# A fused linear-attention and expert layer: one count-table fill moved behind the last unit, the gate weights loaded later, the first expert's weights loaded once

## The chip, the cores and the metric

The kernel runs on one core of a Trainium2 chip. The metric is the device time of one launch in microseconds (us); lower is better. The core has a matrix engine (TensorE, PE in the profile), VectorE (DVE), ScalarE (ACT), GpSimd (POOL) and SyncE (SP). SP and POOL also start transfers; POOL starts all that need an address from a register or from a list of rows.

## The reference

Gated linear attention over 4 sequences of 768 steps and 8 heads of size 48, then a layer of 8 experts on the 3072 tokens (384 numbers each), each expert taking exactly 384 tokens.

```python
# attention
for t in range(S):
    state = alpha[:, :, t, :, None] * state + einsum('bhd,bhe->bhde', k[:, :, t], v[:, :, t])
    y[:, :, t] = einsum('bhd,bhde->bhe', q[:, :, t], state)
# experts: the largest logits first, one expert a token, cap = N / E tokens an expert
logits = x @ w_gate
for idx in argsort(-logits.flatten()):
    tok, e = idx // E, idx % E
    if assigned[tok] < 0 and counts[e] < cap: assigned[tok] = e; counts[e] += 1
for e in range(E):
    out[assigned == e] = relu(x[assigned == e] @ w1[e]) @ w2[e]
```

## The kernel before

**Attention.** The work is cut into 24 units: 6 chunks of 128 steps of each of 4 sequences, all 8 heads in a unit. `loads(n)` brings in alpha, k, q and v of unit n on SP's queue (L345 to L348). In `unit(n)` VectorE runs a product scan over alpha backwards (L366, then a reciprocal, L368) and forwards (L371) and multiplies k by the one (L376); q is multiplied by the other (L381), by VectorE in unit 0 and by GpSimd in all later units. TensorE transposes the scaled k (L394), makes the scores (L404), k times v (L418) and the two products of the output (L442: the carried state, and the scores with v). ScalarE copies the scores out of PSUM (L408) in two halves, `sm`, of four heads each, and GpSimd sets the future half of each to zero (L410). ScalarE copies out the output (L457), and TensorE makes its 8 logits with `wg` and `sel` (L463, L468). Unit 0 is worked in two halves. A few products on zeros (L266) run at the start.

**Choice of tokens.** Instead of sorting, the kernel finds in 7 rounds the expert that fills next and the smallest logit that still gets in: a logit is split in 5 digits (7, 7, 6, 6 and 6 bits), and for each digit VectorE compares all tokens' digits with a ramp (L712, into a count table `cmp`, two buffers `cbuf`, 128 columns a digit value), TensorE counts (L695, L700), and VectorE picks the digit (L698, L703). A digit of 6 bits fills 64 of the 128 columns, yet the counting products read all 128, so that the rest has to hold numbers. `round_(i)` ends in `ei`, the number of expert i (L746), and in a list of its tokens (L837 to L847), with which GpSimd gathers their rows (L854).

**Experts.** Each float32 number is worked as a high and a low part in fp32r, with three products in place of one: high by high, low by high and high by low (L961 for w1, L992 for w2). A quarter of an expert's weights (`g` = 0 to 3, 768 KB, w1 in the first half of its columns and w2 in the second) is loaded by two transfers on GpSimd's queue: `hi` (L875) writes the rounded number, ScalarE writes its negative into the place of the low part in two halves (L885), and `low` (L889) loads the same 768 KB again and adds it to that. ffn1 has to wait for `hi` for its first two products and for `low` for its third. Two sets of buffers take turns (`WS`). The second set lies where the attention's output was.

**What sets the order.** Every step is an `op` with an engine, an estimated length, a due time and what it has to follow; `plan` sorts them once, when the program is built, and each engine then works its list strictly in that order. So a step that waits holds up all that stands behind it on its engine. GpSimd's list mixes transfers, masks and products; SP's holds the loads.

The constants (ramps, shifts, masks, the tables `iotas`, `ramp_b`) are made by the lists `INIT` and `LATE`; there GpSimd fills both `cbuf` with zeros (L322, six steps). For the first expert `second(0)` writes its own order, `hi` and `low` by turns, behind the gathers.

## Time and profile before

| | |
|---|---|
| time, median of 3 runs | 412.94 us (412.81 to 415.25) |
| the profiled execution's own time | 415.02 us |
| its span, first to last instruction | 413.0 us |
| PE, DVE, ACT, POOL busy | 383.0, 258.3, 173.5, 186.1 us |
| mean granted TensorE clock, as a share of the full one | 0.966 |

The rows come from the profiled execution, which is 2.1 us above the median. Times in rows count from its first instruction. Attention takes the first 113 us, the first choice of tokens and the handover go to 147, and the experts to the end. A granted clock of 1.00 is 2.4 GHz, 0.50 is 1.2 GHz.

### The profile page before, as it was taken

To read this page: it belongs to the slowest core of one execution; us is meant where nothing else is said; L and a number is where in the kernel's file an instruction comes from. 1 tells how busy PE (TensorE), PEld (TensorE's weight loads), DVE (VectorE), ACT (ScalarE), POOL (GpSimd) and SP (SyncE) were. 2 spreads that over 40 slices of the span, in tenths; PEclk is the share of its full clock that TensorE was granted. 3 is DMA by queue.
4 is the path that set the end of the run, shared out by engine and by line. 5 is a ranking of instruction groups with operands and counts; after the bars stand their busy time and mean duration, and the time that the engine had idled before them with its cause. 6 is when DMAs were issued, how large, how long until landed. Compare 5 with 4: busy or idle time off the path is not lost.

```text
span 413.0 us, 10416 instructions
## 1 busy us (share of the span) xinstructions
PE 383.0 (93%) x4166; PEld 341.1 (83%) x4166; DVE 258.3 (63%) x649; ACT 173.5 (42%) x320; POOL 186.1 (45%) x271
## 2 busy tenths in 40 slices
PE   6699999999989758899999999999999999999991
PEld 3578787878767447799999999999999999999990
DVE  7699999995557854656956955956865753221110
ACT  4255555556464133424362552551461372553110
POOL 9777876678400421611550660560550473431202
PEclk9699999999998986899999999999999999999997
DMA  7996878940054579998999989889889899999101
GB/s 204 391 340 201 259 236 273 289 136 5 4 193 172 151 202 253 255 306 174 288 283 215 303 201 211 256 235 207 230 267 201 220 326 208 322 272 195 64 0 57
DMA packets 30176, 88.82 MB, mean 215 GB/s; under 512 B 4144, under 2 KB 10544, under 8 KB 30128
## 3 DMA queue, kind: packets, MB, share of 16 engines
q0 software_dynamic: 12288, 59.78, 56.2%
q1 hardware_dynamic: 17840, 28.39, 20.6%
q8 instruction: 32, 0.52, 0.5%
q14 instruction: 16, 0.13, 0.1%
HBM read 78.72 MB, written 9.44 MB: 213 GB/s over the span
## 4 chain that ended last, share of the span: by engine, by line
PE 74%; issue 8%; POOL 5%; DVE 5%; DMA 4%; ACT 1%; POOLq 0%; ACTq 0%
PE h L961 20%; PE y L992 20%; PE y L442 9%; PE s L404 6%; PE xt L695 6%; DMA wset<-in_w_dram 4%; PE xt L394 2%; PE xt L418 2%; PE xt L463 2%; PE xt L928 2%; PE xt L468 2%; POOL out_dram L1006 1%; PE xt L843 1%; POOL cmp L322 1%; DVE hot L837 1%
## 5 line engine op out<-in xcount | busy, mean ns | idle before, releaser
L992 PE MATMUL y<-wset,hh 128*128 128x384 f32 x384 | 102.8, 349 | 0.0
L961 PE MATMUL h<-xh,wset 128*128 128x384 f32 x384 | 92.3, 350 | 5.7 <-DMA wset<-in_w_dram 5.7
L972 ACT ACTIVATE hh<-h 128x384 fp32r<-128x384 f32 x64 | 31.4, 490 | 120.1 <-PE h L961 107.5
L974 DVE SCALAR_TENSOR_TENSOR hl<-h,hh 128x384 fp32r<-128x384 f32 x64 | 35.5, 554 | 65.1 <-ACT hh L972 64.8
L961 PEld LDWEIGHTS h<-xh,wset 128*128 128x128 f32 x384 | 68.9, 193 | 7.1 <-issue 5.0
L992 PEld LDWEIGHTS y<-wset,hh 128*128 128x128 f32 x384 | 68.2, 191 | 0.0
L992 PE MATMUL y<-wset,hl 128*128 128x384 f32 x192 | 65.1, 339 | 0.0
L885 ACT ACTIVATE wset<-wset 128x768 fp32r<-128x768 f32 x64 | 50.7, 839 | 15.1 <-DMA wset<-in_w_dram 14.8
L875 POOL DMA_DIRECT2D wset<-in_w_dram x32 | 21.0, 670 | 67.7 <-PE h L961 39.6
L854 POOL DMA_INDIRECT xr<-x_dram,idx x24 | 25.7, 1070 | 53.9 <-DVE dig L786 27.5
L889 POOL DMA_DIRECT2D wset<-in_w_dram x32 | 29.7, 1154 | 40.5 <-ACT wset L885 39.6
L961 PE MATMUL h<-xl,wset 128*128 128x384 f32 x192 | 45.7, 346 | 0.0
L410 POOL TENSOR_SCALAR_AFFINE_SELECT sm<-sm 128x512 f32<-128x512 f32 x48 | 32.9, 702 | 19.8 <-ACT sm L408 16.6
L1006 POOL DMA_INDIRECT out_dram<-yo,idx x24 | 27.2, 1134 | 30.5 <-ACT yo L1000 22.1
L695 PEld LDWEIGHTS <-cmp 128*128 128x128 bf16 x816 | 30.2, 118 | 10.2 <-DVE cmp L712 5.8
L992 PEld LDWEIGHTS y<-wset,hl 128*128 128x128 f32 x192 | 36.5, 190 | 0.0
L408 ACT ACTIVATE sm<-s 128x512 f32<-128x512 f32 x48 | 26.9, 596 | 18.6 <-PE s L404 17.7
L961 PEld LDWEIGHTS h<-xl,wset 128*128 128x128 f32 x192 | 34.3, 192 | 0.0
L712 DVE TENSOR_TENSOR cmp<-nd,iota 128x1536 bf16<-128x1536 bf16 (+2 forms) x32 | 32.7, 1032 | 1.0
L381 POOL TENSOR_TENSOR qh<-qr,ga 128x512 f32<-128x512 f32 x23 | 29.8, 1295 | 4.8 <-issue 1.8
L695 PE MATMUL xt<-oc,cmp 128*128 128x8 bf16 x720 | 28.9, 175 | 2.3 <-DVE cmp L712 2.3
L442 PE MATMUL y<-sm,vr 128*48 128x128 f32 x384 | 26.8, 283 | 4.0 <-POOL sm L410 4.0
(160 smaller groups left out, 579.1 us busy)
## 6 DMA issues: line engine op xcount, KB each, us to landing
wset<-in_w_dram POOLq DMA_DIRECT2D x64, 768.0 KB, 9.1
kr<-in_k_dram SPq DMA_DIRECT2D x24, 256.0 KB, 4.5
qr<-in_q_dram SPq DMA_DIRECT2D x24, 256.0 KB, 4.6
al<-in_alpha_dram SPq DMA_DIRECT2D x23, 258.5 KB, 4.2
vr<-in_v_dram SPq DMA_DIRECT2D x24, 192.0 KB, 3.5
x_dram<-xga SPq DMA_DIRECT2D x24, 192.0 KB, 1.9
xr<-x_dram,idx POOLq DMA_INDIRECT x24, 3.8
out_dram<-yo,idx POOLq DMA_INDIRECT x24, 6.5
```

The source lines that it names most:

```text
L381: (V if n == 0 else G).tensor_mul(qh[:, ps_], qr[:, ps_], ga[:, lo:hi].rearrange("p (g x) -> p g x", x=C1)[:, :, 1:])
L410: op("POOL", 0.65, lambda h=h: G.affine_select(sm[:, h], sm[:, h], pattern=[[0, HP], [1, C]], compare_op=OP.is_ge, fill=0.0, base=0, chann ...
L442: P_.matmul(yv[64 * g:64 * g + D, h, s], lhs, rhs, start=(h, g) not in fresh, stop=last and s == 1, skip_group_check=True)
L695: P_.matmul(rt_c, cmp_[:, j // U, :, j % U], o[:, j], start=j == 0, stop=j == NU - 1, skip_group_check=True)
L712: x = op("DVE", (1.75 if nt == 128 else 0.95) / n + 0.03, lambda js=js: V.tensor_tensor(words(cbuf[t % 2], nt, js), keyed(d, nt, js), each ...
L885: pre.append(op("ACT", 0.84, lambda hs=hs: A.activation(WS[i % 2][:, 1, g][:, hs], WS[i % 2][:, 0, g][:, hs].bitcast(F32), AF.Copy, scale= ...
L889: accs[i, g] = op("POOL", 0.92, lambda: nc.gpsimd.dma_start(WS[i % 2][:, 1, g], w12.bitcast(F32R)[bass.ds(eng_reg[i], 1), :, g].rearrange( ...
L961: P_.matmul(o, WS[i % 2][:, a, g, c0 + d * 128:c0 + (d + 1) * 128], x[:, d], start=m_ == 0 and d == 0, stop=m_ == 2 and d == DB - 1)
L972: a_ = op("ACT", 0.49, lambda: A.activation(HHT[m], o, AF.Relu), after=[y], r=[("hb", n_)], w=[("hh", n_)], at=at, boost=25, lat=0.1)
L974: op("DVE", 0.54, lambda: V.scalar_tensor_tensor(HLT[m], o, 0.0, HHT[m], op0=OP.max, op1=OP.subtract), after=[a_], r=[("hb", n_), ("hh", n ...
L992: P_.matmul(YB[b][:, :Dm], a[:, bs], w, start=q == 0 and n == 0, stop=q == FB - 1 and n == 2)
L1006: st_ = nc.gpsimd.indirect_dma_start(out=out, out_offset=bass.IndirectOffsetOnAxis(ap=IDX[i][:, b:b + 1], axis=0), in_=YO[c % 5], in_offse ...
```

## The change

Six things are changed.

1. The six fills of `cbuf` at the start are gone. One fill, of columns 64 to 127 of the first buffer, stands behind the masks of the last unit. (The second buffer's first use writes all 128 columns.)
2. The two loads of `wg` stand behind the loads of unit 1 on SP's queue, as a step of their own.
3. In unit 0 q is multiplied by GpSimd too, and k ahead of the forward scans; the products of its two score halves with v are two steps.
4. The tables `iotas` and `ramp_b` are made by VectorE elsewhere: `iotas` in units 0 and 1, `ramp_b` behind the scaled k of unit 6.
5. For the first expert each quarter is loaded once, as it is, into one of four new buffers (`RAW`); ScalarE writes the high part from it (two halves), and VectorE subtracts to make the low part (two halves). The halves are separate steps, so that w1's products do not wait for w2's half. All other experts are loaded as before. The first expert's four transfers stand in a row.
6. Estimated lengths of loads and fills are changed in the planner, which moves other steps by places.

```diff
+WG_AT, Q_DVE, K0_AT = -1.4, (), -0.05
+BY_DVE = ((0, 1, 2, 3), ())
...
     def wgate():
         V.memset(wg, 0.0)
+        V.tensor_reduce(sel, ident.rearrange("p (i e) -> p e i", e=32)[:, :E], axis=X_, op=OP.add)
+
+    def wgate_load():
         for h in range(2):
             nc.sync.dma_start(wg[64 * h:64 * h + D, :, :E],
                               w_gate.rearrange("(b h d) e -> h d b e", h=2, d=D)[h])
...
+    c_wg = op("DVE", 0.3, wgate, at=-4.0)
+    op("SP", 0.87, wgate_load, after=[c_wg], w=[("wg", 0)], at=WG_AT, dma=1.0, lat=1.0)
...
-    for c_ in cbuf:
-        for w_ in range(0, NW, 2):
-            LATE.append(("POOL", 0.6, lambda c_=c_, w_=w_: G.memset(c_[:, w_:w_ + 2], 0.0)))
...
-                (V if n == 0 else G).tensor_mul(qh[:, ps_], qr[:, ps_],
+                (V if n in Q_DVE else G).tensor_mul(qh[:, ps_], qr[:, ps_],
...
+    op("POOL", 1.45, lambda: G.memset(cbuf[0][:, :, 64:], 0.0), after=lastw["sm", NU - 1], at=NU + 5.0)
...
         def hi(g, after, follow=()):
...
+            raw = g in BY_DVE[i > 0]
...
+            x = op("POOL", 0.58, lambda: nc.gpsimd.dma_start(
+                t, w12[bass.ds(eng_reg[i], 1), :, g].rearrange("e p f -> p (e f)")), after=after, follow=follow,
+                w=[("raw", k)], at=at, dma=2.0, lat=LH if i else 0.5)
+            for h in range(2):
+                hs = slice(h * WB // 2, (h + 1) * WB // 2)
+                his[i, g, h] = op("ACT", 0.84, lambda hs=hs: A.activation(WS[i % 2][:, 0, g][:, hs], t[:, hs], AF.Copy),
...
+            for h in range(2):
+                hs = slice(h * WB // 2, (h + 1) * WB // 2)
+                accs[i, g, h] = op("DVE", 0.87, lambda hs=hs: V.tensor_sub(
+                    WS[i % 2][:, 1, g][:, hs], t[:, hs], WS[i % 2][:, 0, g][:, hs].bitcast(F32)),
...
     def second(i):
         hi, low, x = late_w.pop()
         rows = [gathers[i, NB - 1]]
-        if i == 0:
-            for g in range(GP):
-                hi(g, [x], rows)
-                rows = [his[0, g]]
-                if g:
-                    low(g - 1, rows)
-                    rows = [accs[0, g - 1]]
-            low(GP - 1, rows)
...
```

GpSimd's list at the start, before: `cmp` are the two count tables, `sm` the score halves of units 0, 1 and 2, `qh` the scaled q of units 1 and 2.

```order
L318 AFFINE_SELECT tri<-one_82 128x128
L322 MEMSET cmp_96 128x1024 x3
L322 MEMSET cmp_97 128x1024 x3
L410 AFFINE_SELECT sm_152<-sm_152 128x512 x2
L381 TENSOR_TENSOR qh_148<-qr_129,ga_143 128x512
L381 TENSOR_TENSOR qh_149<-qr_130,ga_142 128x512
L410 AFFINE_SELECT sm_153<-sm_153 128x512 x2
```

GpSimd's list at the same place after:

```order
L321 AFFINE_SELECT tri<-one_82 128x128
L381 TENSOR_TENSOR qh_147<-qr_128,ga_142 128x256 x2
L410 AFFINE_SELECT sm_152<-sm_152 128x512 x2
L381 TENSOR_TENSOR qh_148<-qr_129,ga_143 128x512
L410 AFFINE_SELECT sm_153<-sm_153 128x512 x2
L381 TENSOR_TENSOR qh_149<-qr_130,ga_142 128x512
```

The six fills are gone, the two half products of unit 0's q are new, and the masks of unit 1 now stand ahead of unit 2's q.

GpSimd's list at the handover, before, from the third quarter of the first expert on: `wset_1709` is the first expert's set, `wset_2154` the second's, `ei_1726` the second's number; L875 is `hi`, L889 `low`.

```order
L875 DMA wset_1709<-in_w_dram 128x1536
L870 TENSOR_LOAD ei_1726
L870 ISA x2
L875 ISA
L875 DMA wset_2154<-in_w_dram 128x1536
L889 ISA
L889 DMA wset_1709<-in_w_dram 128x1536
L875 ISA
L875 DMA wset_2154<-in_w_dram 128x1536
L889 ISA
L889 DMA wset_1709<-in_w_dram 128x1536
L854 DMA xr_1711<-x_dram,idx_1789 128x384 x3
```

GpSimd's list at the handover after, with `raw` for the new buffers, `wset_2153` for the second expert's set and `xr_1706` for its gathered rows (L907 loads raw, L898 is `hi`, L933 `low`).

```order
L907 DMA raw_1713<-in_w_dram 128x1536
L907 ISA
L907 DMA raw_1714<-in_w_dram 128x1536
L883 TENSOR_LOAD ei_1725
L883 ISA x2
L898 ISA
L898 DMA wset_2153<-in_w_dram 128x1536
L898 ISA
L898 DMA wset_2153<-in_w_dram 128x1536
L867 DMA xr_1706<-x_dram,idx_1788 128x384 x3
L933 ISA
L933 DMA wset_2153<-in_w_dram 128x1536
```

Before, the last two `low` of the first expert stood behind the load of the second expert's number; after, nothing of the first expert does.

VectorE's list in round 1 after, at the first two quarters (before, the rows with `raw` were not there): g, k and nd are the small steps between two digits, `cmp` the compares, `hl` the low parts of hidden values.

```order
L725 TENSOR_TENSOR cmp_96<-nd_1731,iota_78 128x6x256
L917 TENSOR_TENSOR wset_1704<-raw_1711,wset_1704 128x768 x2
L711 TENSOR_SCALAR g_1728<-xt_168 128x8
L917 TENSOR_TENSOR wset_1704<-raw_1712,wset_1704 128x768
L716 TENSOR_REDUCE k_1726<-xt_168 128x1
L747 SCALAR_TENSOR_TENSOR nd_1730<-nd_1731,k_1726,dig_1777 128x24
L725 TENSOR_TENSOR cmp_97<-nd_1730,iota_79 128x6x256
L917 TENSOR_TENSOR wset_1704<-raw_1712,wset_1704 128x768
L1010 SCALAR_TENSOR_TENSOR hl_2158<-h_1715,hh_2154 128x384
```

The new subtractions stand between the small steps of the round: seven of the eight come ahead of `ei` of expert 1.

## Rows read from the trace of the kernel before

**Rows 1.** The page: span, and busy time of each engine.

```profile
span 413.0 us, 10416 instructions
PE 383.0 (93%) x4166; PEld 341.1 (83%) x4166; DVE 258.3 (63%) x649; ACT 173.5 (42%) x320; POOL 186.1 (45%) x271
```

**Rows 2.** Busy time of each engine in stretches; behind them clock, DMA share, GB/s.

```profile
10.00:20.00 10.00, 6.73 (x64) 5.34 (x64) 6.11 (x11) 2.28 (x4) 7.50 (x9) 0.66 1.06 392
30.00:110.00 80.00, 80.00 (x1455) 64.83 (x1454) 70.23 (x108) 45.46 (x93) 59.28 (x77) 1.00 0.57 184
...
150.00:157.00 7.00, 2.40 (x31) 1.97 (x31) 3.07 (x8) 0.69 (x1) 2.08 (x4) 0.68 0.89 196
157.00:163.00 6.00, 6.00 (x42) 5.38 (x41) 2.96 (x17) 2.56 (x4) 0.00 (x0) 0.52 1.06 282
...
171.00:177.00 6.00, 4.18 (x25) 3.96 (x26) 1.47 (x2) 1.33 (x2) 4.85 (x5) 0.72 1.06 280
177.00:381.00 204.00, 203.88 (x1781) 193.45 (x1779) 121.54 (x359) 84.16 (x146) 79.35 (x106) 1.00 0.96 246
```

**Rows 3.** Timeline of the first 25 us: start, length, engine; in brackets idle time before.

```profile
2.36 0.87 SPq L279 DMA_DIRECT2D wg<-in_moe_w_gate_dram  x2
...
6.87 5.41 POOL L322 MEMSET cmp<- 128x1024 bf16 x6
...
6.91 0.77 PE L394 MATMUL xt<-ident,kh 128*128 128x128 f32 x4 [0.97 <-DVE kh L376]
...
8.82 1.08 ACT L408 ACTIVATE sm<-s 128x512 f32<-128x512 f32 x2 [0.51 <-PE s L404]
...
9.16 1.23 DVE L366 TENSOR_TENSOR_SCAN sc<-al,d 128x516 f32<-128x516 f32 x1 [1.30 <-DMA al<-in_alpha_dram]
...
12.23 1.57 POOL L410 TENSOR_SCALAR_AFFINE_SELECT sm<-sm 128x512 f32<-128x512 f32 x2
...
13.27 1.95 PE L442 MATMUL y<-sm,vr 128*48 128x128 f32 x16 [4.00 <-POOL sm L410]
...
16.19 2.08 PE L404 MATMUL s<-qh,kh 64*128 64x128 f32 x16
...
19.68 0.36 DVE L423 COPY st<-xt 128x192 f32<-128x192 f32 x1 [3.75 <-PE xt L418]
```

**Rows 4.** The chain that ended last: scores of unit 4.

```profile
29.29 1.16 PE s L404 x16
```

**Rows 5.** Single lines: durations in ns (shortest, median, longest), first and last start.

```profile
L324 DVE TENSOR_SCALAR iota<-iota x4: 395/652/786, 85.4 to 95.4; 128x256 bf16<-128x256 bf16 x3, 128x512 bf16<-128x512 bf16 x1
L376 DVE TENSOR_TENSOR kh<-kr,sc x25: 399/680/1117, 6.4 to 98.4; 128x512 f32<-128x512 f32 x23, 128x256 f32<-128x256 f32 x2
L381 POOL TENSOR_TENSOR qh<-qr,ga x23: 1171/1184/1634, 13.8 to 103.0; 128x512 f32<-128x512 f32 x23
L885 ACT ACTIVATE wset<-wset x64: 826/838/849, 147.3 to 375.1; 128x768 fp32r<-128x768 f32 x64
```

**Rows 6.** Timeline of the first expert's start.

```profile
147.30 1.58 ACT L885 ACTIVATE wset<-wset 128x768 fp32r<-128x768 f32 x2 [1.86 <-DMA wset<-in_w_dram]
...
147.36 0.77 PE L961 MATMUL h<-xh,wset 128*128 128x384 f32 x3 [1.05 <-DMA wset<-in_w_dram]
...
149.11 1.58 ACT L885 ACTIVATE wset<-wset 128x768 fp32r<-128x768 f32 x2 [0.23 <-DMA wset<-in_w_dram]
149.18 0.92 POOL L889 DMA_DIRECT2D wset<-in_w_dram  x1 [5.77 <-ACT wset L885]
...
156.35 1.30 PE L961 MATMUL h<-xh,wset 128*128 128x384 f32 x3 [2.80 <-DMA wset<-in_w_dram]
...
161.79 0.15 DVE L746 TENSOR_SCALAR ei<-es 128x1 int32<-128x1 f32 x1
...
163.26 0.54 POOL L875 DMA_DIRECT2D wset<-in_w_dram  x1 [10.84 <-DVE m L762]
...
172.82 1.16 PE L961 MATMUL h<-xh,wset 128*128 128x384 f32 x3 [1.82 <-DMA wset<-in_w_dram]
```

More of the change, by code (lines that the diff above doesn't have):

```diff
@@ L348, in fn @@
                     nc.sync.dma_start(t, src[n])
-            op("SP", sz if nm != "v" else 0.7, fn, w=[(nm, n)], at=n - 3.0, lat=2.2)
+            op("SP", 0.84 if nm == "al" and first else 0.4, fn, w=[(nm, n)], at=n - 3.0,
+               dma=(0.68 if nm != "v" else 0.5) * (1.6 if n < 2 else 1.0), lat=1.3)
     def unit(n):
@@ L444, in go, with within @@
             fresh.add((h, g))
-        def within():
-            for h in range(2):
+        def within(hs=(0, 1)):
+            for h in hs:
                 for p in range(HP):
@@ L453, in unit @@
                at=n + 0.75, take="Y")
-        op("PE", 0.9, within, shape=48, r=[("v", n), ("sm", n), ("pads", 0)] + ([("Y", n)] if c else []),
-           w=[("Y", n)], banks=("Y",), at=n + 0.8, take=None if c else "Y")
+        if n == 0:
+            sm0, sm1 = (lastw["sm", n][j::2] for j in range(2))
+            x = op("PE", 0.45, lambda: within((0,)), shape=48, r=[("v", n), ("pads", 0)], after=sm0, w=[("Y", n)],
+                   banks=("Y",), at=n + 0.8, take="Y")
+            op("PE", 0.45, lambda: within((1,)), shape=48, after=[x] + sm1, r=[("v", n), ("sm", n)], w=[("Y", n)],
+               banks=("Y",), at=n + 0.8)
+        else:
+            op("PE", 0.9, within, shape=48, r=[("v", n), ("sm", n), ("pads", 0)] + ([("Y", n)] if c else []),
+               w=[("Y", n)], banks=("Y",), at=n + 0.8, take=None if c else "Y")
         yt = YT[n]
@@ L606, in gla_moe_kernel @@
     RX = 4
+    raws = [0]
+    RAW = [wp.tile([128, WB], F32, name=f"raw{j}") for j in range(4)]
     HHT, HLT, YO = [], [], []
@@ L880, in low @@
         def low(g, rows):
-            at = start(i) + 2 * g * TE / FB - (9 if i else 0)
-            pre = [his[i, g]]
+            if g in BY_DVE[i > 0]:
+                return
+            at = low_at(g)
+            pre = [his[i, g, 0]]
             for h in range(2):
@@ L899, in second @@
         rows = [gathers[i, NB - 1]]
-        if i == 0:
-            for g in range(GP):
-                hi(g, [x], rows)
-                rows = [his[0, g]]
-                if g:
-                    low(g - 1, rows)
-                    rows = [accs[0, g - 1]]
-            low(GP - 1, rows)
-        else:
-            for g in range(FIRST_HI[min(i, 2)], GP):
-                hi(g, [x], rows)
-            for g in range(GP):
-                low(g, rows)
+        for g in range(FIRST_HI[min(i, 2)], GP):
+            hi(g, [x], rows)
+        for g in range(GP):
+            low(g, rows)
     prepped = {}
```

59 lines of the change are left out of this document (37 added, 22 removed).

## The prediction

> **What bounds the kernel now.** I read the page first: TensorE is busy for 383.0 of 413.0 us [rows 1], so a gain has to come from the 30 us in which it is idle or from stretches in which its clock is low. Then the stretches [rows 2]. From 30 to 110 us TensorE is busy for all of 80.00 us at full clock, from 177 to 381 for 203.88 of 204.00. In both, whatever the other engines save is worth nothing, and a delay at the start of either is passed on whole to the end. Two places are left.
>
> *The head.* In 10 to 20 us TensorE is busy for 6.73 of 10 at a granted clock of 0.66 [rows 2]. The timeline says why: the first scores are copied from 8.82 on, but GpSimd fills the count tables from 6.87 for 5.41 us, and its mask of unit 0 starts only at 12.23; TensorE has then waited 4.00 us and starts its products at 13.27 [rows 3]. It comes back at the lower of its two levels, 1.2 GHz: unit 1's scores take 2.08 us, where unit 4's take 1.16 [rows 3, 4]. VectorE had run ahead and then stood for 3.75 us, up to 19.68, for a product of the late TensorE [rows 3].
>
> *The first expert.* In 150 to 157 TensorE is busy for 2.40 of 7 us; in 157 to 163 always, but at a clock of 0.52; in 171 to 177 for 4.18 of 6 at 0.72 [rows 2]. The waits are for the second load of a quarter: issued at 149.18 because ScalarE first had to write the negative, landed only when TensorE goes on at 156.35, 7.2 us later; and again at 172.82 [rows 6]. Before that last one GpSimd stood for 10.84 us, because the load of expert 1's number (made at 161.79) is ahead of it in its list [rows 6].
>
> How much is lost there: idle 4.60 in 150 to 157 and 1.82 in 171 to 177; at half speed 6.00 x 0.48 = 2.9 in 157 to 163, 6 x 0.28 = 1.7 in 171 to 177, and some 0.3 before 157. Together 11.3 us.
>
> **The change part by part: the head.** *Fills.* The six fills end 5.41 us of GpSimd's start. The new one has 6 x 64 x 4 columns in place of twelve thousand; it stands behind unit 23's masks, where GpSimd has nothing to do until the gathers, and the table is first read two digits later. If that cover were gone it would cost its own length, between 0.7 (an eighth of 5.41, by its columns) and twice that. I take 0.
>
> *Unit 0.* k now comes ahead of the forward scans, which lets the transposes start about 1.0 earlier than 6.91 [rows 3]. q is GpSimd's: two halves of some 0.6 (half of the 1.18 of a whole unit [rows 5]), against two of 0.4 on VectorE. They end at about 8.2, the scores at about 9.0 to 9.4, the first masked half at 10.3, the second at 11.0, and the products with v, now in two steps, at 11.5 in place of 15.2 (13.27 + 1.95 [rows 3]).
>
> *Gate weights.* Their two loads (0.87 of SP's time [rows 3]) stood ahead of unit 0's q and v; VectorE waited 1.30 us for unit 1's alpha [rows 3]. Moving them is worth between 0 and 1.3 by itself; I take that it only lets VectorE start unit 1 when it is free. The loads queued behind them now are unit 2's; logits of unit 0 need the weights at about 12.5, and by the present spacing they land by 11.
>
> *Tables on VectorE.* The four `iotas` (0.40 to 0.79 each [rows 5], together 2.2) move from where VectorE had slack (85 to 95 us) into units 0 and 1, `ramp_b` (about as long as one of the larger) from the start to unit 6. This is the price of the head: VectorE is there the engine that feeds TensorE. Its unit 1 starts at about 8.3 (9.16 before [rows 3]), unit 3 at about 16.1, where before it waited until 19.68 plus 0.3. From there it takes 3.3 us a unit as before; unit 4's forward scan ends at 22.0, its q at 23.4, and its scores at 25.2 in place of 30.45 (29.29 + 1.16 [rows 4]). TensorE has then done about the same other products as before at 30.45, so the lead is 5.2 us. Behind it TensorE is the bound, needing over 4 us a unit, and keeps the lead to the end of attention and, since the choice of tokens is listed as before, to the handover.
>
> **The first expert.** All times in this part are those of the present trace, without that lead. *Removed:* four second loads that add, with the wait for ScalarE in front of each. *Loads.* The four raw loads start where `hi` starts now; the first lands at 147.3, and the next 1.81 us later, as the rows of ScalarE show (147.30 and 149.11 [rows 6]). So the last of four lands at about 152.8; now the last part needed comes past 177.
>
> The Trainium skill says otherwise in DMA: Bandwidth & Descriptors, section Where 436 GB/s comes from: transfers between HBM and SBUF are held by the HBM side at about 358 GB/s a core, by which 768 KB takes an estimated 2.2 us. By it the last quarter lands 1.2 later and the sum below is smaller by at most that; the spacing of 1.81 in this trace is shorter, so the trace does not agree.
>
> *ScalarE.* As many steps as before, of the same shape: 8 of 0.84 [rows 5]. But they now stand ahead of the first product: the first half is ready at 148.2, so TensorE starts 0.85 later than 147.36 [rows 6]. The halves follow the landings at 1.6 a quarter, faster than they land.
>
> *VectorE.* Eight subtractions of 768 columns are new. No row has this shape; the product with k has two float32 inputs in SBUF as well, 0.40 for 256 columns and 0.68 for 512 [rows 5], which gives 0.96 for 768 and 7.7 in all. The other end is the slowest such row, 1.12 for 512, so 1.68 and 13.4 in all. I take 0.96, because the median is at 0.68. They cannot bring a gain. In 150 to 163 VectorE is busy for only 6.03 of 13 us [rows 2], so that most of it fits. Seven of them stand ahead of `ei` of expert 1; against that, the counting products of round 1 no longer wait behind TensorE's idle time. Replaying the list, I get `ei` at about 161, hardly other than 161.79.
>
> *What is late next.* Two things. TensorE, no longer held by transfers, catches up with VectorE's chain of round 1: the first table of round 2 comes about 1.0 too late for its place. And expert 1: its first `hi` can't go out before its number is known (163.26 now [rows 6]), three gathers follow, then the first `low`, which by the 7.2 of the present one lands at about 179 to 180; TensorE wants it at about 180.4. I take 0.5 for that. Everything else of expert 1 lands 3 to 8 us ahead.
>
> Sum: 11.3 - 0.85 - 1.0 - 0.5 = 9.0.
>
> *The clock.* Both sums take full clock. But the head still has idle stretches of about 1.3 and 0.5, and ahead of the first expert's product there is now about 1.9 in place of 1.05 [rows 6]. The rows show half clock behind an idle time of 4.00 and behind a stretch with 4.6 idle of 7, and none behind 0.97 [rows 2, 3]; what lies between is not shown. One fall loses 1.7 or more (in 171 to 177). I take one fall and a part of a second, 2.2.
>
> **Forecast.** 5.2 + 9.0 - 2.2 = 12.0. Against the profiled execution's own time 415.02 - 12.0 = 403.0 (its span would be 401.0); it is 2.1 above the median, and the gain taken from the median gives 412.94 - 12.0 = **400.9 us**, rounded to 401. That is the forecast, with 399 to 403.5 as its own range.
>
> **The rivals.** *No fall of the clock.* Both places keep 1.00 throughout: 412.94 - 14.2 = 398.7; with the gate weights' 1.3 on top 397.5. For it: the 0.97 of idle without a fall. Against: the stretch from 139 to 147 was already full of waits.
>
> *The subtractions lengthen round 1.* At 1.68 each, seven in front of `ei` are 5.0 dearer, expert 1's first `low` is that much later and TensorE waits for it as it waits now at 156.35: 400.9 + 5.0 = 405.9. For it: they stand between small steps each of which waits for TensorE. Against: VectorE's idle time there.
>
> *Only the head.* The loads of the first expert are no longer the bound but expert 1's are: `ei` comes no earlier, and the wait moves there. If all of the 9.0 were lost so, 412.94 - 5.2 + 2.2 = 409.9, a gain still under 1%. Against: the second `low` of expert 1 is ahead by several us in the list.
>
> *Slower.* The same mechanism, further: `ei` of expert 1 would have to come some 14 us later than 161 before expert 1's wait eats both gains, because each us of it beyond the half us of slack costs TensorE one. Eight subtractions would then have to take over 2.6 each on VectorE, and no row is above 1.12 for two thirds of the size. It would give 413 to 417.
>
> *The change doesn't do what it says.* The raw loads still stand behind the gathers, so that expert 0 starts no earlier; if the copies were no faster than the second loads, only the head would be left, as above.
>
> **How the numbers follow.** Forecast 0.55, no fall 0.15, longer round 1 (and any mixture that ends between 403.5 and 408.5) 0.21, only the head and the like (within 1%, which is about what a measurement of this kernel can tell from no change: 408.8 to 417.1) 0.06, slower by over 1% 0.03. The range has to leave out no more than 2 in 10: from 397.5 (no fall, with the gate weights) to 406.5, which takes in the dear subtractions. Faster by over 1%: 0.55 + 0.15 + 0.21 = 0.91; same 0.06; slower 0.03.
>
> **What would show it.** In the changed profile: no fill ahead of the first mask, which starts before 10; unit 4's scores end near 25; attention ends 4 to 5 us earlier; the four raw loads land within 6 us of each other, TensorE's idle time for `wset` is gone; subtractions of 0.9 to 1.0; first products of expert 1 with no long wait. I am wrong if GpSimd's or VectorE's list holds TensorE at the head for more than 2 us, if the subtractions take over 1.3, if expert 1's first `low` comes more than 2 us late, or if the clock is low for over 7 us in either place.

## The result, and the profile after

The changed kernel takes **407.56 us** (median; 406.67 to 409.4) against 413.09 for the kernel before, a ratio of 0.9874 with a 95% interval of 0.9841 to 0.9907. So it is faster, by 5.5 us and not by 12: 401 was forecast, and 407.56 lies 1.1 above the range. Of the profiled executions used below, that of fills_only (423.26 us, its kernel's median 419.62) is a slow one of its kernel.

The page of the execution profiled after, which has a time of its own of 406.81 us (it answers to [rows 1]):

```profile
span 405.1 us, 10417 instructions
PE 382.0 (94%) x4166; PEld 340.1 (84%) x4166; DVE 265.9 (66%) x655; ACT 173.6 (43%) x320; POOL 180.7 (45%) x264
```

The timeline of the head after (it answers to [rows 3] and [rows 4]):

```profile
9.54 1.22 POOL L410 TENSOR_SCALAR_AFFINE_SELECT sm<-sm 128x512 f32<-128x512 f32 x2 [1.48 <-ACT sm L408]
...
10.23 1.23 PE L442 MATMUL y<-sm,vr 128*48 128x128 f32 x16 [1.41 <-POOL sm L410]
...
12.57 1.16 PE L404 MATMUL s<-qh,kh 64*128 64x128 f32 x16
...
24.84 1.16 PE L404 MATMUL s<-qh,kh 64*128 64x128 f32 x16
```

The first mask starts at 9.54 in place of 12.23, the wait of 4.00 has become 1.41, unit 1's scores take 1.16 in place of 2.08, and unit 4's end at 26.00 in place of 30.45. The lead of 4.5 is carried whole to the end of attention (the last product of unit 23), 108.56 in place of 113.24.

The start of the first expert after (it answers to [rows 6]):

```profile
142.82 1.58 ACT L912 ACTIVATE wset<-raw 128x768 fp32r<-128x768 f32 x2 [0.67 <-DMA raw<-in_w_dram]
...
143.71 0.80 PE L997 MATMUL h<-xh,wset 128*128 128x384 f32 x3 [0.68 <-ACT wset L912]
...
144.42 1.82 DVE L917 TENSOR_TENSOR wset<-raw,wset 128x768 fp32r<-128x768 f32 x2
...
144.64 1.58 ACT L912 ACTIVATE wset<-raw 128x768 fp32r<-128x768 f32 x2 [0.24 <-DMA raw<-in_w_dram]
```

The long waits for a second load (2.80 at 156.35, 1.82 at 172.82) are gone. The first product comes at 143.71, 3.65 earlier than before: of the head's lead about one us is not there any more. What is still lost is seen best in stretches, from one event to another that both kernels have. The first row is the head up to the scores of unit 4, the second goes from the end of attention to the first expert product, the third from there to the last product of the third expert (columns as in [rows 2]). The kernel before:

```profile
0.00:30.46 30.46, 23.07 (x242) 15.96 (x244) 23.43 (x39) 12.95 (x24) 23.80 (x59) 0.89 0.91 312
113.24:147.36 34.12, 27.49 (x320) 21.55 (x321) 23.96 (x84) 13.31 (x29) 4.80 (x5) 0.95 0.55 189
147.36:262.31 114.95, 108.35 (x1008) 100.61 (x1009) 74.25 (x234) 44.98 (x75) 42.85 (x54) 0.94 0.94 236
```

The changed kernel, with the first expert alone as a fourth row:

```profile
0.00:26.00 26.00, 20.97 (x255) 14.06 (x255) 23.12 (x39) 13.12 (x24) 18.98 (x54) 1.00 0.97 339
108.56:143.71 35.15, 29.40 (x320) 23.36 (x320) 23.61 (x84) 14.22 (x30) 5.79 (x7) 0.85 0.55 190
143.71:254.40 110.69, 107.82 (x1008) 99.67 (x1009) 80.58 (x241) 44.09 (x74) 37.38 (x48) 0.97 0.82 214
143.71:188.11 44.40, 42.38 (x398) 38.60 (x399) 33.49 (x87) 18.17 (x30) 9.88 (x12) 0.92 0.62 175
```

Head 4.46 shorter, handover 1.03 longer, three experts 4.26 shorter; from the fourth expert on nothing changes. That is 7.7 of the 7.9 by which the spans differ. In the first expert 2.02 us of idle time are left, and the clock of 0.92 costs TensorE about 42.38 x 0.08 = 3.4.

Where that idle time comes from, the chain of waits shows (start, length, what):

```profile
170.31 9.36 DMA wset<-in_w_dram
...
179.71 0.73 issue
180.44 0.83 ACT wset L929
181.27 0.39 ACT hh L1008
...
181.68 0.56 DVE hl L1010
182.23 0.09 DVE g L711
...
182.36 0.17 PE xt L713
```

and the timeline of the same place, with the idle times:

```profile
175.97 0.95 PE L708 MATMUL xt<-oc,cmp 128*128 128x8 bf16 x24 [0.80 <-DVE cmp L725]
...
179.69 1.58 ACT L929 ACTIVATE wset<-wset 128x768 fp32r<-128x768 f32 x2 [3.99 <-DMA wset<-in_w_dram]
...
181.68 0.56 DVE L1010 SCALAR_TENSOR_TENSOR hl<-h,hh 128x384 fp32r<-128x384 f32 x1 [2.62 <-ACT hh L1008]
...
182.36 0.17 PE L713 MATMUL xt<-g,one 128*128 128x8 bf16 x1 [1.17 <-DVE g L711]
182.38 0.91 PE L997 MATMUL h<-xh,wset 128*128 128x384 f32 x3
```

Read upwards: TensorE waits 1.17 for a small step of VectorE, `g`. That stands in VectorE's list behind the low part of a hidden value, which waits 2.62 for ScalarE's high part. ScalarE had been ready for it, but ahead of it in its list is the negation of the third quarter of **expert 1**, and the load for that, issued at 170.31, lands at 179.66. So one load of the next expert stops TensorE on the first expert, by way of ScalarE and VectorE. Behind the wait the product of 0.77 takes 0.91 and the next ones 1.16: the clock is at half.

### The profile page after: what moved, and what is told of

Its sections match the earlier page's. It is cut to its first block, busy times and chain, and to the rows that moved or that the text cites. A ratio compares the mean times of both kernels' runs of the same rounds, so it can differ in the third digit from the quotient of the medians.

```text
span 405.1 us, 10417 instructions
## 1 busy us (share of the span) xinstructions
PE 382.0 (94%) x4166; PEld 340.1 (84%) x4166; DVE 265.9 (66%) x655; ACT 173.6 (43%) x320; POOL 180.7 (45%) x264
## 4 chain that ended last, share of the span: by engine, by line
PE 68%; issue 9%; DMA 8%; DVE 7%; POOL 3%; SPq 1%; ACT 1%; POOLq 0%; ACTq 0%
PE h L997 19%; PE y L1028 16%; PE y L442 8%; PE s L404 6%; PE xt L708 6%; DMA wset<-in_w_dram 5%; PE xt L394 2%; PE xt L470 2%; PE xt L418 2%; PE xt L475 2%; PE xt L964 2%; POOL out_dram L1042 1%; DMA vr<-in_v_dram 1%; DMA kr<-in_k_dram 1%; SPq L347 1%
## 5 line engine op out<-in xcount | busy, mean ns | idle before, releaser
L997 PE MATMUL h<-xh,wset 128*128 128x384 f32 x384 | 90.8, 346 | 0.7 <-ACT wset L912 0.7
L929 ACT ACTIVATE wset<-wset 128x768 fp32r<-128x768 f32 x56 | 44.7, 839 | 24.1 <-DMA wset<-in_w_dram 24.0
L898 POOL DMA_DIRECT2D wset<-in_w_dram x28 | 18.5, 663 | 77.2 <-DVE m L775 45.0
L997 PE MATMUL h<-xl,wset 128*128 128x384 f32 x192 | 46.8, 353 | 0.0
L1042 POOL DMA_INDIRECT out_dram<-yo,idx x24 | 25.8, 1077 | 34.5 <-ACT yo L1036 29.5
L933 POOL DMA_DIRECT2D wset<-in_w_dram x28 | 26.6, 1251 | 24.0 <-ACT wset L929 23.1
L381 POOL TENSOR_TENSOR qh<-qr,ga 128x512 f32<-128x512 f32 (+1 forms) x25 | 33.2, 1328 | 7.1 <-DVE ga L371 2.7
L371 DVE TENSOR_TENSOR_SCAN ga<-al,d 128x516 f32<-128x516 f32 (+1 forms) x25 | 29.5, 1181 | 1.7
```

What stands on the lines that cost most here:

```text
L371: V.tensor_tensor_scan(ga[:, lo:hi], a[:, lo:hi], dps[:, lo:hi], 1.0, op0=OP.mult, op1=OP.add)
L381: (V if n in Q_DVE else G).tensor_mul(qh[:, ps_], qr[:, ps_], ga[:, lo:hi].rearrange("p (g x) -> p g x", x=C1)[:, :, 1:])
L929: pre.append(op("ACT", 0.84, lambda hs=hs: A.activation(WS[i % 2][:, 1, g][:, hs], WS[i % 2][:, 0, g][:, hs].bitcast(F32), AF.Copy, scale= ...
L997: P_.matmul(o, WS[i % 2][:, a, g, c0 + d * 128:c0 + (d + 1) * 128], x[:, d], start=m_ == 0 and d == 0, stop=m_ == 2 and d == DB - 1)
L1042: st_ = nc.gpsimd.indirect_dma_start(out=out, out_offset=bass.IndirectOffsetOnAxis(ap=IDX[i][:, b:b + 1], axis=0), in_=YO[c % 5], in_offse ...
```

## The experiments

Two theories for the missing 6.5 us stood against each other. **A**: TensorE is idle less, as forecast, but it gives time back in new stretches of low clock, which fall elsewhere in each execution. **B**: the waits for expert 0's loads are replaced by waits for expert 1's, through ScalarE's list. Each run is compared with the kernel before on its own chip, by ratio: the kernel before took 412.7 to 412.9 on two chips here and 420.0 to 421.9 on three others, so microseconds are not compared across them.

### The same kernels again

No edit. 

> The kernel before, unchanged, run several times and profiled once more, because the execution that was profiled (415.02) lies 2.1 above the median. Theory A (that execution had one stretch of low TensorE clock more than most): a median of 412.8 to 413.4, with single times 2 us or so apart, and a second profile in which one or two of the low stretches (128.7, 152.6 to 162.8, 173.1) are missing, shorter or elsewhere, so that idle time and lost clock from 147 to 198 come to some 10 us in place of 11.9. Rival (the profiler's own cost): the same low stretches at the same places, and the difference of 2 us lies outside the rows.

> The changed kernel, unchanged, profiled once more and timed in five rounds. Theory A (low stretches of the clock fall at other places from one execution to the next, and are worth 1.7 us each): median 407 to 408.3, single times spread over 2 to 3 us, and the second profile has the same idle times but other low stretches between 115 and 190. Rival (the order of the lists alone sets the time): the spread is under 1 us and the low stretches lie where they lay, at 121 to 128, 138 to 142, 145 to 149 and 183 to 186.

> The changed kernel, unchanged, as the measure for the three runs beside it: 5 to 6 us under the kernel before on the same chip (ratio 0.987 to 0.989), with waits of 0.8, 1.1 and 0.8 us in the first to third expert and 3 to 5 us of lost clock in each of handover and first expert.

> The changed kernel, unchanged, as the measure for the three runs beside it: a ratio of 0.982 to 0.989 to the kernel before on the same chip, the waits in the first three experts and the lost clock as in its other profiles.

> The changed kernel, unchanged, as the measure for the run beside it: ratio 0.983 to 0.992 to the kernel before on the same chip.

Measured: before_again 413.47 us, ratio 1.0007 (0.9972 to 1.0041), its profiled execution 412.98 with a span of 411.4. Its three stretches:

```profile
0.00:29.62 29.62, 23.03 (x242) 16.62 (x244) 23.43 (x39) 12.95 (x24) 23.44 (x59) 0.83 0.93 324
112.40:146.97 34.57, 28.16 (x320) 22.36 (x321) 24.24 (x84) 13.37 (x29) 4.97 (x5) 0.90 0.56 191
146.97:260.75 113.78, 107.72 (x1008) 99.91 (x1009) 73.94 (x234) 45.04 (x75) 42.79 (x54) 0.96 0.95 237
```

The head is 0.84 shorter and the three experts 1.17 than in the first profile, with the same lists. So two of the 12 us were not there to be won in this execution. Only a part of that is A, though: the head's 0.84 is idle time (7.39 before, 6.59 here, at a lower clock), because unit 1's alpha lands earlier and VectorE waits 0.60 for it in place of 1.30; of the experts' 1.17 about half is idle time and half busy time.

The changed kernel's ratio was 0.9891 (after_again), 0.9825 (after_ref), 0.9916 (after_ref2) and 0.9760 (after_ref3). Where the kernel before takes 412.7 to 412.9 the ratios are 0.9891 and 0.9916, a gain of 4.5 and 3.5; where it takes 420 and more, 0.9825 and 0.9760, a gain of 7.4 and 10.1. After_again's stretches:

```profile
0.00:26.54 26.54, 21.40 (x255) 14.29 (x255) 23.44 (x39) 13.18 (x24) 19.05 (x54) 1.00 0.95 333
109.11:144.68 35.57, 29.20 (x321) 23.51 (x321) 24.44 (x85) 14.31 (x30) 5.58 (x7) 0.84 0.55 192
144.68:254.71 110.03, 108.06 (x1008) 99.99 (x1009) 80.02 (x240) 43.92 (x74) 37.60 (x48) 0.96 0.82 214
```

The handover has again a clock of 0.84. Single times of the changed kernel spread over 1.4 to 5.8 us, by the run, as A expected and more. Its other half did not come true: the low stretches lie nearly where they lay. In all five profiles of the changed kernel the clock is 0.50 from 123 to 126 us and between 0.50 and 0.70 from 147 to 150, and one more low stretch comes in the later part of the first expert, between 177 and 189.

### Each half of the change alone

head_only: the changed attention part, the first expert loaded as before.

```diff
-BY_DVE = ((0, 1, 2, 3), ())
+BY_DVE = ((), ())
     def second(i):
+        if i == 0:
+            for g in range(GP):
+                hi(g, [x], rows)
...
```

> The changed attention part (fills, gate weights, unit 0, tables) with the first expert loaded as before, by hi and low. The trace after shows a lead of 4.7 us at the end of attention. If it is passed on whole: 413.1 - 4.7 = 408.4, about all of what the whole change gave. If low stretches of the clock in the choice of tokens eat part of it (5.0 us lost there after, 1.7 before): 410 to 411.7. The first expert's waits are then as before, some 10 to 12 us of idle time and lost clock.

raw_only: attention part, constants, fills and the planner's lengths of loads of before, the new loading of the first expert.

> The attention part as before, with the first expert's weights loaded raw. The trace after has 5.85 us less from the first product to the end of the first expert, and gives 1.75 of it back up to the third expert. If that holds here too: 413.1 - 0.3 - 4.1 = 408.7 or so. If the kernel before loses 2 us less there in most executions than in the profiled one: 410.7. If expert 1's loads take back the rest: 412 to 413.

Measured on one chip: head_only 409.85, ratio 0.9934 (0.9898 to 0.9970); raw_only 411.20, ratio 0.9966 (0.9937 to 0.9994); both halves together (after_again) 0.9891. So the head brings some 2.7 us and the raw loads 1.4, which add up to 4.1 of 4.5, with intervals of 1.2 to 2.4 us to either side. Handover and three experts of head_only, and then of raw_only:

```profile
108.61:142.20 33.59, 26.36 (x320) 20.25 (x321) 23.64 (x84) 13.21 (x29) 5.03 (x5) 1.00 0.55 189
142.20:255.24 113.04, 106.94 (x1008) 99.28 (x1009) 74.50 (x234) 44.97 (x75) 42.95 (x54) 0.95 0.96 241
```

```profile
111.59:146.73 35.14, 29.33 (x321) 23.61 (x320) 24.43 (x85) 14.32 (x30) 5.52 (x7) 0.84 0.55 189
146.73:189.93 43.20, 41.65 (x396) 37.95 (x397) 32.27 (x84) 16.18 (x26) 9.39 (x11) 0.93 0.61 174
146.73:257.90 111.17, 107.16 (x1008) 99.09 (x1009) 80.07 (x240) 44.18 (x74) 37.48 (x48) 0.97 0.81 214
```

Raw loads make the first expert 5.9 to 7.1 shorter (43.20; 50.25 and 49.08 in the two profiles of before), but the three experts together only 2.6 to 3.8 (111.17 against 113.78 and 114.95): 3.3 are given back in the second and third expert (2.5 as idle time). This is B, in a kernel without the head's change. The wait is of the same kind, only longer; the load is the fourth quarter's, issued at 175.06:

```profile
189.55 0.84 ACT L919 ACTIVATE wset<-wset 128x768 fp32r<-128x768 f32 x1 [4.68 <-DMA wset<-in_w_dram]
...
190.80 0.56 DVE L1000 SCALAR_TENSOR_TENSOR hl<-h,hh 128x384 fp32r<-128x384 f32 x1 [3.58 <-ACT hh L998]
...
191.48 0.17 PE L703 MATMUL xt<-g,one 128*128 128x8 bf16 x1 [1.55 <-DVE g L701]
```

### Parts of the head

fills_only: the kernel before without its six fills, with the one fill behind the last unit.

```diff
-    for c_ in cbuf:
-        for w_ in range(0, NW, 2):
-            LATE.append(("POOL", 0.6, lambda c_=c_, w_=w_: G.memset(c_[:, w_:w_ + 2], 0.0)))
...
+    op("POOL", 1.45, lambda: G.memset(cbuf[0][:, :, 64:], 0.0), after=lastw["sm", NU - 1], at=NU + 5.0)
```

> The kernel before, with only the six fills taken from the start and one fill behind the last unit. If the fills alone set the head: GpSimd's first mask starts near 9.5 in place of 12.23, the wait of 4.00 falls to about 1.3, no low clock in unit 1, and unit 4's scores end near 26 to 27, so 412.9 - 3 to 4, 409 to 410. Rival (VectorE, which waits for alpha behind the gate weights and does q of unit 0, is the next bound): unit 4's scores end near 28.5, 411 to 412.

Measured: 419.62, ratio 0.9960 (0.9926 to 0.9995). The timeline:

```profile
9.49 1.23 POOL L407 TENSOR_SCALAR_AFFINE_SELECT sm<-sm 128x512 f32<-128x512 f32 x2 [2.57 <-ACT sm L405]
...
10.18 1.23 PE L439 MATMUL y<-sm,vr 128*48 128x128 f32 x16 [0.91 <-POOL sm L407]
...
13.16 1.09 PE L391 MATMUL xt<-ident,kh 128*128 128x128 f32 x4 [1.75 <-DVE kh L373]
```

The mask comes as early as in the full change and the wait of 4.00 becomes 0.91, yet in this execution unit 4's scores end at 30.44, no earlier than before. What follows the products with v is late: TensorE waits 1.75 for unit 1's k and then runs at half clock (the granted clock of 0 to 30.44 us is 0.83). That product for k takes 1.64 on VectorE, in place of 0.68 before: GpSimd, which no fill holds any more, works its product for q over the same time, from 11.29 to 12.47. So here taking the fills away moves the wait to VectorE. By the times, fills_only gains 0.4% and head_only 0.7%, with intervals that overlap, on two chips: that the other edits of the head add to the fills is likely from the rows, and not shown.

wg_ahead: the changed kernel with the gate weights' loads back between k and q of unit 0.

```diff
-WG_AT, Q_DVE, K0_AT = -1.4, (), -0.05
+WG_AT, Q_DVE, K0_AT = -3.5, (), -0.05
-    c_wg = op("DVE", 0.3, wgate, at=-4.0)
+    c_wg = op("DVE", 0.9, wgate, at=-4.0)
```

> The changed kernel with the two loads of the gate weights back at their place of before, between k and q of unit 0 on SP's queue. All loads behind them are issued 0.87 later. If that place was part of what the head gained: VectorE waits about 0.9 for alpha of unit 1, the scores of unit 4 end near 27 and the lead of 4.5 falls to 3.3 to 3.7, time 1 us over the changed kernel. Rival (VectorE is busy with the tables then and does not wait): no difference that can be told.

Measured: 409.97, ratio 0.9917 (0.9888 to 0.9946), beside 0.9916 of the changed kernel on that chip: no difference. VectorE waits only 0.26 for unit 1's alpha, with all four `iotas` now in front of it in its list, and unit 4's scores end at 25.88. The rival held. But the edit moved other steps too: six transposes of the output (1.3 us) now stand ahead of the end of attention, TensorE waits 0.43 and 0.26 where the changed kernel does not, and attention ends at 110.42. So the run does not price the place by itself. That leaves k ahead of the forward scans, q on GpSimd and the order of loads for the rest of the head's lead; they were not taken apart.

### Expert 1's loads and ScalarE's list

hi_early, and hi_early_2 on another chip: all four `hi` of expert 1 ahead of its gathers.

```diff
-FIRST_HI = (0, 2, 4)
+FIRST_HI = (0, 4, 4)
```

> The changed kernel, with all four hi loads of expert 1 ahead of the gathers of its tokens on GpSimd's queue, in place of two. In the trace after, ScalarE's list has the hidden values of the first expert behind the negation of expert 1's third quarter, which waits 3.99 us for a load that lands at 179.66; VectorE then waits 2.62 for ScalarE, TensorE 1.17 for VectorE, and a low stretch of the clock follows. If that chain is what was lost: the third and fourth quarters land at 167 to 170, the 2 us of idle time in the first expert and the low stretch at 183 go, and the time is 407.5 - 2 to 3.5, 404 to 405.5. Rival: the gathers are now behind two more loads (3.7 us), and TensorE waits for the tokens of expert 1 instead: 407 to 409.

> The changed kernel with all four hi loads of expert 1 ahead of its gathers, once more, beside the changed kernel on one chip. If the chain load, ScalarE, VectorE, TensorE was what was lost in the first and second expert: 2 to 3.5 us under the changed kernel. If TensorE waits for the tokens of expert 1 instead (0.92 in the first run of this kernel, where 1.17 and 0.80 were): within 1 us of the changed kernel.

Measured: ratio 0.9772 (0.9726 to 0.9817), and 0.9787 (0.9737 to 0.9838) beside 0.9825 (after_ref) on the same chip. That is 1.2 us less in the medians (411.90, 413.12), inside the spread. Both profiles of this kernel have a handover some 2 us longer with the same lists there (37.24 in hi_early_2, 34.99 in after_ref), which may hide a gain in the experts (112.53 and 113.87). The wait behind ScalarE is gone from the first expert, and the next one stands there (hi_early_2):

```profile
174.38 0.55 PE L964 MATMUL xt<-ident,xr 128*128 128x128 f32 x3 [1.31 <-DMA xr<-x_dram,idx]
...
180.22 0.93 PE L708 MATMUL xt<-oc,cmp 128*128 128x8 bf16 x23 [0.80 <-DVE cmp L725]
```

late_neg: the planner is told that expert 1's `hi` land 6 us later, so that hidden values go first on ScalarE.

```diff
-                    lat=LH if i else 0.5)
+                    lat=(LH + 6.0 * (i == 1)) if i else 0.5)
```

> The changed kernel, with the planner told that expert 1's hi loads land 6 us later, so that it puts the hidden values of the first expert ahead of the negations on ScalarE; the loads themselves are issued as before or a little other. If the order of ScalarE's list makes the wait of 1.17 (and the 0.80 before it): both go, 407.5 - 2 to 3.5, 404 to 405.5. Rival: the negations, and with them the second loads of expert 1, come later, and TensorE waits for these: 407 to 410.

Measured: ratio 0.9827 (0.9776 to 0.9877), beside 0.9772 of hi_early on that chip. The rival: the second loads come later (the first is issued at 172.26 in place of 169.69), and TensorE waits for one of them, twice as long as it had waited for the list:

```profile
182.60 1.33 PE L997 MATMUL h<-xh,wset 128*128 128x384 f32 x3 [2.43 <-DMA wset<-in_w_dram]
```

raw_e1, raw_e1_all and raw_e1_front: two quarters of expert 1 loaded raw as well; all four; all four, three of them ahead of the gathers. The edit of raw_e1_all is shown; raw_e1 has `(2, 3)` for the new part, raw_e1_front `FIRST_HI = (0, 4, 4)` besides.

```diff
-BY_DVE = ((0, 1, 2, 3), ())
+BY_DVE = ((0, 1, 2, 3), (0, 1, 2, 3), ())
-            raw = g in BY_DVE[i > 0]
+            raw = g in BY_DVE[min(i, 2)]
...
```

> The changed kernel with the third and fourth quarter of expert 1 loaded raw as well (one load in place of two; four more subtractions of 0.95 on VectorE). If what the second and third expert give back (0.7 to 3.3 us, by the run) is the queue of expert 1's loads, which hold GpSimd's queue for 3.7 a second load: the waits of TensorE in the first to third expert go, 407.5 - 1.5 to 3, 404.5 to 406. Rival: the subtractions hold up VectorE's rounds, and TensorE waits for its tables: 407 to 409.

> The changed kernel with expert 1 loaded raw as well: its four quarters take one load each in place of two (some 7.5 us of transfers in place of 22), and VectorE makes eight more low halves of 0.95. If the transfers of expert 1 hold TensorE from the end of the first expert to the third (0.8 to 1.5 us of idle time at each of three waits behind ScalarE's negations, with a low stretch of the clock): these waits go, and the time is 2 to 4 us under the changed kernel. Rival: VectorE's rounds get longer by 7.6 us and TensorE waits for the tables instead: the same as the changed kernel or up to 3 us more.

> Expert 1 loaded raw, and three of its four loads ahead of the gathers of its tokens. If the transfers of expert 1 and ScalarE's list behind them are what the first three experts still lose beside the clock: no wait of TensorE for ScalarE's negations up to the third expert, the first three experts together 2 to 3 us shorter than in the changed kernel's profile, and the time 1.5 to 3 us under it. Rival: the tokens of expert 1 come later behind the third quarter (1.9 us), TensorE waits for them, and the time is within 1 us of the changed kernel.

Measured, each beside the changed kernel on its chip: raw_e1 0.9810 (0.9768 to 0.9853) beside 0.9825; raw_e1_all 0.9877 (0.9847 to 0.9907) beside 0.9916; raw_e1_front 0.9837 (0.9793 to 0.9881) beside 0.9760, 3.1 us more in the medians. With expert 1 raw the first expert ends sooner still (42.28 in raw_e1_front against 44.65 in after_ref3), but the three experts together take 115.59 against 112.13: TensorE then waits for the low part of expert 2's tokens (0.63), for a table (0.80) and again for `g` (1.91; 1.42 at the same place in after_ref3). No version is clearly faster than the changed kernel; the best, with all of expert 1 raw, gains 1.6 us by the ratios (0.9877 and 0.9916), inside the intervals.

### The handover

spins: seven more products on zeros there, six more behind the token numbers, two behind each digit of the first choice.

```diff
-SPIN0, SPIN1 = (3,) * 6, (4, 4)
+SPIN0, SPIN1, SPINC = (3,) * 8, (6, 6, 3), 2
...
+        if i == 0:
+            for _ in range(SPINC):
+                op("PE", 0.17, lambda: spin2(1, XB), after=[x], at=prio, small=True, take="X", give="X")
```

> The changed kernel with more products on zeros in TensorE's idle time: two behind each digit of the first choice of tokens, six more behind the token numbers and seven more while the first expert's tokens and weights land. Theory A (TensorE loses some 8 us in 115 to 190 because its clock falls to half after stretches with gaps): the low stretches between 119 and 150 go or shrink, lost clock up to the end of the first expert falls from 8.4 to 9.5 us to under 4, and the time is 403 to 404.5. Rival: the fillers stand ahead of the counting products and delay the chain of the choice, or the low stretches come all the same: 407 to 410.

no_fillers: none at all (`SPIN0, SPIN1 = (), ()`). It leaves out only these products.

> The changed kernel without the 26 products on zeros that stand in TensorE's gaps between the token numbers and the first expert's products (4.4 us of busy time). If TensorE's clock falls there because of the gaps, and the fall costs: a low stretch of 7 us and more between 131 and 155, lost clock in handover and first expert 2 to 4 us more, time 2 to 4 us over the changed kernel. Rival: the fillers themselves stand in the way, or the clock falls all the same: the same time, or up to 1 us less.

Measured: spins 416.94, ratio 0.9927 (0.9899 to 0.9955), slower than hi_early and late_neg on its chip (0.9772, 0.9827); no_fillers 409.26, ratio 0.9928 (0.9899 to 0.9957) beside 0.9916, the same. With more products the clock fell in the choice all the same (0.50 from 123 to 126) but was 1.00 from 132 to 147, where the profile after has 0.59 to 0.84 from 138 to 147; the first expert product came 39.42 us after attention in place of 35.15. Without any, no_fillers shows for its handover

```profile
108.57:143.69 35.12, 24.32 (x295) 20.09 (x295) 24.38 (x85) 14.14 (x30) 5.88 (x7) 0.82 0.55 192
```

with 5 us less of TensorE work, a clock of 0.82 and the same length. So these 5 us of products are not on the chain that ends last, and **the mean clock of the handover does not give its length**. Theory A as it stood, that each low stretch is worth half of it, falls for the handover.

A low stretch there is not free either. TensorE also transposes the last of the attention's output (L655) in the choice, ScalarE copies it (L559), SP stores it, and in eighteen of the twenty profiles the first gather of tokens goes out 1.14 or 1.15 us behind the landing of the last store. The raw loads stand behind the gathers. The longest handover of the changed kernel, after_ref2, beside after, from the transposes on:

```profile
108.52:145.28 36.76, 30.67 (x320) 24.80 (x320) 23.48 (x84) 14.31 (x30) 6.80 (x7) 0.81 0.53 182
...
128.18 1.95 PE L655 MATMUL h<-ident,yta 128*128 128x128 f32 x10
...
130.61 0.49 ACT L559 ACTIVATE xga<-y 128x384 f32<-128x384 f32 x1
...
134.34 2.65 POOL L867 DMA_INDIRECT xr<-x_dram,idx  x1 [27.21 <-DVE oc L801]
```

```profile
128.05 1.40 PE L655 MATMUL h<-ident,yta 128*128 128x128 f32 x10
...
129.93 0.49 ACT L559 ACTIVATE xga<-y 128x384 f32<-128x384 f32 x1
...
133.75 1.17 POOL L867 DMA_INDIRECT xr<-x_dram,idx  x1 [26.59 <-DVE chu L800]
```

The clock from 128 to 130 us is 0.61 there and 0.92 in after; the transposes take 0.55 longer, the copy comes 0.68 later and the gather 0.59 later, which then itself takes 1.5 longer. No run sets the clock, so how much of the spread comes this way is not shown.

raw_early: the raw loads ahead of the first expert's gathers (`FIRST_HI = (4, 2, 4)`).

> The changed kernel with the four raw loads ahead of the gathers of the first expert on GpSimd's queue: they need only its number, made at 126.4, and the gathers wait for the token list until 133.75. If the landing of the raw loads (142.7, first product 143.7) is what holds the start of the first expert: the loads land from 131 to 138, the first product comes at 142 or so, when the tokens are transposed, no wait on ScalarE at its start, and with fewer gaps there fewer low stretches: 407.5 - 1 to 4, 403.5 to 406.5. Rival: the gathers land later behind 3 MB of weights, and the first product waits for the tokens: the same or up to 2 us slower.

Measured: 419.69, ratio 0.9985 (0.9950 to 1.0021): the whole gain is gone. GpSimd's timeline:

```profile
129.41 1.72 POOL L907 DMA_DIRECT2D raw<-in_w_dram  x3 [0.24 <-DVE vi L840]
...
144.31 1.04 POOL L867 DMA_INDIRECT xr<-x_dram,idx  x1 [13.18 <-DMA x_dram<-xga]
```

The gathers wait 13.18 us for the last stores of the attention's output, which share the transfer engines with 3 MB of weights: the last of them takes 11.7 us to land, against 4.8 for the slowest in after_ref. The rival named the right victim, the tokens, but not the stores as the way. With all weights there when it starts, the first expert takes 41.47 us at a clock of 1.00, against 44.17 at 0.88 in after_ref on the same chip, though TensorE is idle for 2.07 of it and for 0.80 there. So in the first expert the low clock does cost time.

## Why the prediction was wrong

**Right by its own steps.** The head's mechanism, and most of its size: mask before 10, no low clock in four of five profiles (0.93 in after_ref2), unit 4's scores at 26.00 where 25.2 was said. The four raw loads land 1.85 to 1.89 apart (142.74 to 148.35), near the 1.81 taken from the trace; the estimate of 2.2 by the Trainium skill (DMA: Bandwidth & Descriptors, Where 436 GB/s comes from) did not hold. ScalarE's half ahead of the first product costs 0.97 (from the landing at 142.74 to 143.71) where 0.85 was taken. The subtraction takes 0.948 where 0.96 was taken:

```profile
L917 DVE TENSOR_TENSOR wset<-raw,wset x8: 945/948/951, 144.4 to 167.9; 128x768 fp32r<-128x768 f32 x8
```

The first table of round 2 is 0.80 late where 1.0 was said; `ei` of expert 1 was not delayed; expert 1's first second load made no wait. The new fill takes 1.37 and ends at 107.16, before anything needs it, so that its 0 was right; the size was misread, since the six fills are 6144 columns and not twelve thousand, and the new one is a quarter of them.

**The steps that failed** are two, and both stand in the sum of 9.0. One is "Everything else of expert 1 lands 3 to 8 us ahead". I had checked the landings against TensorE's need alone. The third quarter's `hi` lands at 179.66, in time for TensorE, but ScalarE's negation for it stands ahead of hidden values of the first expert. The shorter the first expert, the earlier those are due, while that load stands behind expert 1's gathers on GpSimd and goes out at 170.31. TensorE's idle time in the three experts (length less busy time) fell from 6.60 and 6.06 us to 2.87 and 1.97, by 3.9, where the sum has 4.60 + 1.82 - 1.0 - 0.5 = 4.9. In raw_only the three experts gain 2.6 to 3.8, where 9.8 was said (the 9.0 and the 0.85 that falls in the handover). The rival "Only the head" had this mechanism, expert 1's loads as the next bound; I gave it and its like 0.06 because I looked for it on GpSimd's queue and not in ScalarE's list.

That this chain is the wait is shown by the rows. That it is the whole of what is missing in the experts is not: moving the loads or the list took that wait away and put another in its place, for 0 to 1.6 us.

The other, and the larger, is the clock. The sum takes all 4.9 us of half speed in the first expert (2.9 + 1.7 + 0.3) as won back, and the forecast takes 2.2 off again for new falls, which leaves 2.7. A low clock shows as longer busy time, and TensorE's busy time for the 1008 products of the three experts was 108.35 and 107.72 before and is 107.82 and 108.06 after: 0.1 less. So the low stretches were moved and not removed. In the first expert of the profile after, the clock is 0.73 from 143.71 to 150 and 0.70 from 182.36 to 188.11, some 1.7 us each; the second lies right behind the 1.17 above, the first behind the waits of the handover. 1.0 and 2.6 are the 3.6 that the experts lack below.

**A step of method that failed.** The losses, 11.3 in the first expert and 5.2 in the head, were read from one execution 2.1 above the median and taken off the median as they stood. The second profile of before has 0.84 less in the head and 1.17 less in the experts, and a third one of the same attention part, raw_only, ends its head at 28.82. A loss that the median execution doesn't have can't be won there.

By stages, means of two profiles each: the head ends 3.8 earlier ((30.46 + 29.62 - 26.00 - 26.54) / 2; 5.2 said), the handover is 1.0 longer (0.85 said; 2.6 above the first profile in after_ref2), the three experts are 4.0 shorter (9.8 said, and 2.2 of clock to be taken off somewhere). 3.8 - 1.0 + 4.0 = 6.8, where the medians show 5.5. So of the 6.5 that are missing the experts with the clock make 3.6, the head 1.4, the handover 0.15, and 1.3 lies between these profiles and the medians: the two executions of before took 414.0 on average, 0.9 above their median, the two of after 406.9, 0.7 below theirs.

**Open.** Which of k's place, q's engine and the loads' order carries the head beside the fills; what part of the first expert's remaining low clock follows from its waits, and how much of the spread from the low stretch in the choice; and why the change is worth twice as much on the chips where the kernel before takes 420 us.

## What to carry to other kernels

When a transfer is taken off the critical path, follow not only when the next data land against the engine that needs them, but every in-order list that a waiting step stands in: a step for the *next* stage, placed ahead by a planner's guess of a landing, blocks the present one. Count a low stretch of the clock as won only when the gaps around it go too; here the busy time stayed. Take a gain off the median only after a second profile of the unchanged kernel, since one execution's idle time and low clock may be its own. And where transfers of two kinds share the engines, bringing the big one forward starves the small one that the chain waits for: 13.18 us here.

## What the runs showed of the hardware that was not expected

- The stretches of low clock are not the same in two executions of one program: the head has a clock of 0.89 and 0.83 in two profiles of before, the handover 0.95 and 0.90 (1.00 in head_only). Yet in five profiles of the changed kernel they come at nearly the same places (0.50 from 123 to 126 in each).
- More products on zeros in the gaps did not keep the clock up in the choice of tokens (0.50 from 123 to 126 in spins), and leaving all of them out cost nothing that can be told (0.9928 and 0.9916).
- VectorE's product for k takes 0.67 alone and GpSimd's for q 1.18. Where they run over each other, the one that starts second is longer: k took 1.64 when it started 0.08 behind q (fills_only, 11.37), and q 1.54 when k was 0.16 ahead (before, 15.42).
- The plain load of 768 KB hardly changed on the slower chips: ScalarE's copies, which wait for the landings, start 1.83 and 1.88 apart in after_ref and 2.11 and 1.89 in after_ref3. Yet the fourth expert took 33.9 us in after_ref3 in place of 32.35 in after_ref2, with a wait of TensorE for VectorE's `g` of 1.37 (and 1.45 in the fifth) that is not there in after_ref2. VectorE starts `g` 1.87 behind the counting product there (302.71) and 0.04 behind it in after_ref2 (300.06). The last two experts, beside which no round runs, take the same time on both chips. What holds VectorE there was not found.
